# Fourier mixing and a squared-ReLU layer: a seven-product scheme for most groups, sums and casts by DMA

## The chip, the cores and the metric

The kernel runs on one core of a Trainium2 chip. The metric is the device time of one launch in microseconds, the median of several runs. The profile shows one execution in detail: TensorE (PE, with its weight loads as PEld), VectorE (DVE), ScalarE (ACT), GpSimd (POOL), SyncE (SP) and the DMA queues.

## The reference

```python
# x: (8, 3008, 256); filt_r, filt_i: (1505, 256); w_in: (256, 2048); w_out: (2048, 256)
def _attn_ref(x, filt_r, filt_i):
    X = np.fft.rfft(x, axis=1)
    F = (filt_r + 1j * filt_i)[None, :, :]
    return np.fft.irfft(X * F, n=x.shape[1], axis=1).astype(np.float32)

def _moe_ref(x, w_in, w_out):                     # x: the result above, 24064 rows of 256
    h = np.maximum(x @ w_in, 0.0)
    return (h * h @ w_out).astype(np.float32)
```

Each of the 8 sequences is filtered in the frequency domain, and the 24064 rows that result go through two layers with the square of a ReLU between them.

## The kernel before

The discrete Fourier transform of 3008 = 64 x 47 points is made of matrix products with constant matrices in f16. For each sequence `b` it runs in steps: `unit_a` (16 units: transforms of 47 points), a way out to DRAM and back that changes the layout (`write_u`, `read_u`), `unit_b` (12 units: transforms of 64 points, times the filter), `unit_p` (12 units: back), again through DRAM (`read_z`), and `unit_y` (16 units), which leaves the filtered sequence in `yts`. x comes in as f32 and is cast to f16:

```python
def load_x(b, c, pool=None, tag="x32", q=None):
    t = (pool or p_x32).tile([96, 8, D], F32, tag=tag, name=f"x32_{b}_{c}")
    q = q or nc.sync
    ...
    x32s[(b, c)] = t

def cast_x(b, c, eng=nc.vector):
    t = p_x16.tile([94, 8, D], F16, tag="x16", name=f"x16_{b}_{c}")
    eng.tensor_copy(out=t, in_=x32s.pop((b, c))[0:94])
    x16s[(b, c)] = t
```

`unit_b` multiplies each pair of rows by both parts of the filter. `prod[:, 0]` and `prod[:, 1]` are the two halves of the complex product; the second has to be added with its upper and lower 64 partitions exchanged:

```python
def unit_b(b, p):
    ps = psF(...)                                   # psF: a ring of two PSUM banks
    for i in range(2):
        nc.tensor.matmul(ps[:, i * D:(i + 1) * D], sSB[:, 2 * p + i, :],
                         uts[b][:, 2 * p + i, :], start=True, stop=True)
    prod = p_prod.tile([128, 2, 2, D], F16, tag="prod", name=f"prod_{b}_{p}")
    nc.vector.tensor_mul(out=prod, in0=<ps, each element twice>, in1=sF[:, :, 2 * p:2 * p + 2, :])
    if b > 0:
        yf = p_yf.tile([128, 2, D], F16, tag="yf", name=f"yf_{b}_{p}")
        nc.vector.tensor_copy(out=yf[0:64], in_=prod[64:128, 1])
        nc.vector.tensor_copy(out=yf[64:128], in_=prod[0:64, 1])

def unit_s(b, p):
    prod, yf = prods[(b, p)]
    nc.vector.tensor_add(out=yf, in0=prod[:, 0], in1=yf)

def unit_p(b, p):
    ps = psF(f"psP_{b}_{p}")
    for i in range(2):
        nc.tensor.matmul(ps[:, i * D:(i + 1) * D], sSP[:, 2 * p + i, :], yf[:, i, :], start=True, stop=True)
    nc.scalar.copy(out=zes[(b, c)][:, 2 * i6:2 * i6 + 2, :], in_=ps...)
    ...
```

The two layers run in 47 groups of 512 rows, each in 8 slots. In slot `s` of group `g` the first layer makes two of its 16 blocks of `h2` (2048 x 512, f16), ScalarE takes the ReLU out of PSUM and VectorE squares it; beside this the second layer of the group before is computed, and units of the Fourier part are strewn in by a plan:

```python
def ffn_g1(g, s):
    for i in range(2):
        jt = 2 * s + i
        ...
        nc.tensor.matmul(ps[:, i, o:o + n], sWin[:, dt, jt * 128:(jt + 1) * 128], yts[b][:, dt, r:r + n], ...)
    nc.scalar.activation(out=h2[:, 2 * s:2 * s + 2, :], in_=ps, func=AF.Relu)

def ffn_sq(g, s):
    v = h2s[g][:, 2 * s:2 * s + 2, :]
    nc.vector.tensor_mul(out=v, in0=v, in1=v)

def ffn_g2(g, s):                                   # direct: 8 products of 256 columns a slot
    t, half = divmod(s, 2)
    for jt in range(8 * half, 8 * half + 8):
        nc.tensor.matmul(pso[g][:, t % 2, :], h2s[g][:, jt, t * 128:(t + 1) * 128],
                         sWout[:, jt, :], start=(jt == 0), stop=(jt == NJT - 1))
```

For groups 40 to 45 the second layer uses Strassen's scheme in Winograd's form instead: h2 and w_out are seen as 2 x 2 blocks, four sums of blocks of h2 (`sums`, in slots 0, 1, 2 and 4) and four of w_out (`make_t`, once) leave seven block products in place of eight. `products` computes them in parts over the 8 slots, 14 matmuls of 128 columns in each on average, and puts the results together:

```python
def sums(g, k):                                     # k = 0, 1, 2, 4
    t = p_x16.tile([128, 8, D], F16, tag="x16", name=f"sum_{g}_{k}")
    if k == 0:
        nc.vector.tensor_add(out=t, in0=a21, in1=a22)
    ...

def products(g, k):
    for p, m0, m1 in PARTS[k]:
        ...
        for m in range(m0, m1):
            q, t = divmod(m, 2)
            nc.tensor.matmul(o[:, t, :], f[p][:, q, 128 * t:128 * t + 128], sg["w"][p][:, q, :], ...)
        if p == 1:
            f["pu"] = p_prod.tile([128, 2, 2, 128], F32, tag="prod", name=f"pu_{g}")
            nc.scalar.copy(out=f["pu"][:, 0], in_=o)
        ...
        elif p == 2:
            nc.vector.tensor_add(out=f["top"][:, :, 0:128], in0=f["y"][:, 0], in1=f["pu"][:, 0])
            nc.vector.tensor_add(out=f["bot"][:, :, 128:256], in0=f["y"][:, 1], in1=f["pu"][:, 1])
        ...
        elif p == 3:
            nc.vector.tensor_add(out=f["top"][:, :, 128:256], in0=o, in1=f["u2"])
            store(g, 0, 2, f["top"])
```

The plan of a sequence (`b` > 1; `first` is a multiple of 8 slots) and the loop:

```python
t0 = 6                                              # unit_a: two a slot, slots 6 to 13
put(14, 1, read_u, b)
t0 = 19
for p in range(12):                                 # unit_b: 12 over 19 slots, unit_p two slots later
    r = t0 + 18 * p // 11
    put(r, 0, unit_b, b, p)
    put(r, 0, unit_s, b, p)
    put(r + 2, 1, unit_p, b, p)
for c in range(4):
    put(40, 1, read_z, b, c)
...                                                 # load_x and cast_x of the next sequence
for n in range(16):                                 # unit_y: two a slot, slots 45 to 52
    put(45 + n // 2, n % 2, unit_y, b, n)

SEVEN = range(40, NG - 1)
for s in range((NG + 1) * SLOTS):
    g, k = divmod(s, SLOTS)
    if g < NG: ffn_g1(g, k)
    run(work, s, 0)
    if (s - 1) // SLOTS - 1 in SEVEN: products((s - 1) // SLOTS - 1, (s - 1) % SLOTS)
    if g > 0 and g - 1 not in SEVEN: ffn_g2(g - 1, k)
    run(work, s, 1)
    ...
    if g - 1 in SEVEN: sums(g - 1, k)
    if g < NG: ffn_sq(g, k)
```

Of the kernel before, what the change touches and what calls it, by code (L numbers as in the profile page):

```python
# [110 lines left out]
def kernel(  # L111
# [32 lines left out]
    p_prod = ctx.enter_context(tc.tile_pool(name="p_prod", bufs=3))  # L144
    p_yf = ctx.enter_context(tc.tile_pool(name="p_yf", bufs=4))
# [3 lines left out]
    p_out = ctx.enter_context(tc.tile_pool(name="p_out", bufs=3))  # L149

# [33 lines left out]
    x32s = {}  # L184

    def load_x(b, c, pool=None, tag="x32", q=None):

        t = (pool or p_x32).tile([96, 8, D], F32, tag=tag, name=f"x32_{b}_{c}")
        q = q or nc.sync
        if b + 1 < B:  # L190
            v = xrows[b * S:b * S + 96 * NM, :].rearrange("(p m) d -> p m d", m=NM)
            q.dma_start(out=t, in_=v[:, 8 * c:8 * c + 8, :])
        else:
            v = xrows[b * S:b * S + S, :].rearrange("(p m) d -> p m d", m=NM)
            q.dma_start(out=t[0:80], in_=v[0:80, 8 * c:8 * c + 8, :])
            q.dma_start(out=t[80:94], in_=v[80:94, 8 * c:8 * c + 8, :])
        x32s[(b, c)] = t
# [3 lines left out]
    sC0 = const.tile([128, 1472], F16, name="sC0")  # L201
# [3 lines left out]
    sSA = sC0[0:94, 1280:1376]  # L205
    sSY = sC0[0:112, 1376:1470]
# [40 lines left out]
    nc.sync.dma_start(out=sC0[:, 704:1472], in_=dC0.ap()[:, 704:1472])  # L247
# [60 lines left out]
    def load_win():  # L308

        for k, c, n, pool, tag in ((0, 0, 768, p_ze, "ze"), (0, 768, 768, p_ze, "ze"),  # L310
                                   (0, 1536, 512, p_prod, "prod"), (1, 0, 768, p_ze, "ze"),
                                   (1, 768, 512, p_prod, "prod"), (1, 1280, 512, p_prod, "prod"),
                                   (1, 1792, 256, p_yf, "yf")):
            t = pool.tile([128, n], F32, tag=tag, name=f"win32_{k}_{c}")
            nc.sync.dma_start(out=t, in_=moe_w_in[128 * k:128 * k + 128, c:c + n])
            wins.append((t, k, slice(c, c + n)))
# [19 lines left out]
    x16s, us, uts, prods, zes, zts, yts = {}, {}, {}, {}, {}, {}, {}  # L336

    def cast_x(b, c, eng=nc.vector):
        t = p_x16.tile([94, 8, D], F16, tag="x16", name=f"x16_{b}_{c}")
        eng.tensor_copy(out=t, in_=x32s.pop((b, c))[0:94])  # L340
        x16s[(b, c)] = t

# [5 lines left out]
    def unit_a(b, a):  # L348

        c, i = divmod(a, 4)  # L350
        if i == 0:
            us[(b, c)] = p_u.tile([96, 8, D], F16, tag="u", name=f"u_{b}_{c}")
        ps = psF(f"psA_{b}_{a}")
        m = slice(2 * i, 2 * i + 2)
        if b == 1:
            nc.tensor.matmul(ps[0:96, :], s1[:, c // 2, :], xw16[(b, 2 * (c % 2))][:, m, :],
                             start=True, stop=False)
            nc.tensor.matmul(ps[0:96, :], s1[0:120, 2 + c, :], xw16[(b, 1)][0:120, m, :],
                             start=False, stop=True)
        else:  # L360
            nc.tensor.matmul(ps[0:96, :], sSA, x16s[(b, c)][:, m, :], start=True, stop=True)  # L361
        o = us[(b, c)][:, 2 * i:2 * i + 2, :]
        pv = ps[0:96, :].rearrange("p (a d) -> p a d", d=D)
        if a % 2 == 0:
            nc.scalar.copy(out=o, in_=pv)  # L365
        else:
            nc.vector.tensor_copy(out=o, in_=pv)  # L367
        if i == 3:
            write_u(b, c)
# [69 lines left out]
    def unit_b(b, p):  # L439
# [18 lines left out]
        if b > 0:  # L458
            yf = p_yf.tile([128, 2, D], F16, tag="yf", name=f"yf_{b}_{p}")
            nc.vector.tensor_copy(out=yf[0:64], in_=prod[64:128, 1])  # L460
            nc.vector.tensor_copy(out=yf[64:128], in_=prod[0:64, 1])
            prods[(b, p)] = prod, yf

    def unit_s(b, p):

        prod, yf = prods[(b, p)]
        nc.vector.tensor_add(out=yf, in0=prod[:, 0], in1=yf)  # L467
        prods[(b, p)] = yf
# [20 lines left out]
    def unit_p(b, p):  # L489
# [3 lines left out]
        yf = prods.pop((b, p))  # L493
# [12 lines left out]
    ztiles = [const.tile([112, 8, D], F16, name=f"zt_{c}") for c in range(4)]  # L506
# [3 lines left out]
    def read_z(b, c, ks=(0, 1)):  # L510
        zt = ztiles[c]
        v = dZ[b].rearrange("(q j) d -> q j d", j=NM)
        for k in ks:
            nc.sync.dma_start(out=zt[64 * k:64 * k + 48],
                              in_=v[48 * k:48 * k + 48, 8 * c:8 * c + 8, :])
        zts[(b, c)] = zt
# [51 lines left out]
    def ffn_sq(g, s):  # L568
        v = h2s[g][:, 2 * s:2 * s + 2, :]
        nc.vector.tensor_mul(out=v, in0=v, in1=v)  # L570
# [46 lines left out]
    def make_t():  # L617

        t = p_x32.tile([128, 4, 8, 128], F16, tag="x32", name="sT")
# [13 lines left out]
    def sums(g, k):  # L633
# [7 lines left out]
        t = p_x16.tile([128, 8, D], F16, tag="x16", name=f"sum_{g}_{k}")  # L641
# [17 lines left out]
    def products(g, k):  # L659

        f = sg[g]
        for p, m0, m1 in PARTS[k]:
# [12 lines left out]
            if p == 1:  # L675
                f["pu"] = p_prod.tile([128, 2, 2, 128], F32, tag="prod", name=f"pu_{g}")
                nc.scalar.copy(out=f["pu"][:, 0], in_=o)
            elif p == 6:
                f["u2"] = p_prod.tile([128, 2, 128], F32, tag="prod", name=f"u2_{g}")
                nc.scalar.copy(out=f["u2"], in_=o)  # L680
            elif p == 7:
                nc.scalar.copy(out=f["pu"][:, 1], in_=o)
            elif p == 2:
                f["top"] = p_out.tile([128, 2, 256], F32, tag="ost", name=f"top_{g}")
                f["bot"] = p_out.tile([128, 2, 256], F32, tag="ost", name=f"bot_{g}")
                nc.vector.tensor_add(out=f["top"][:, :, 0:128], in0=f["y"][:, 0], in1=f["pu"][:, 0])
                nc.vector.tensor_add(out=f["bot"][:, :, 128:256], in0=f["y"][:, 1], in1=f["pu"][:, 1])
            elif p == 4:
                nc.scalar.copy(out=f["bot"][:, :, 0:128], in_=o)
                store(g, 2, 2, f["bot"])  # L690
            elif p == 3:
                nc.vector.tensor_add(out=f["top"][:, :, 128:256], in0=o, in1=f["u2"])
                store(g, 0, 2, f["top"])

    def fft_plan(b):
# [11 lines left out]
        t0 = 2 if b == 1 else 6  # L707
        for a in range(12 if b == 1 else 0, 16):
            put(t0 + a // 2, a % 2, unit_a, b, a)
        put(10 if b == 1 else 14, 1, read_u, b)  # L710
        t0 = 14 if b == 1 else 19
        for p in range(12):
            r = t0 + (17 if b == 1 else 18) * p // 11
            put(r, 0, unit_b, b, p)
            put(r, 0, unit_s, b, p)
            put(r + 2, 1, unit_p, b, p)
        t0 = 34 if b == 1 else 40
        for c in range(4):
            put(t0, 1, read_z, b, c)
        if b + 1 < B:  # L720
            for c in range(2):
                put(t0 - 13, 1, load_x, b + 1, c)
            for c in range(4):
                r = t0 - 8 + 3 * c
                put(r, 1, cast_x, b + 1, c)
                if c < 2:
                    put(r, 1, load_x, b + 1, c + 2)
# [79 lines left out]
    SEVEN = range(40, NG - 1)  # L807
    work = {}
    for b in range(1, B):
        first = (b * S // TG) * SLOTS - (48 if b > 1 else 40)  # L810
        for (r, place), w in fft_plan(b).items():
            work[(first + r, place)] = w
# [49 lines left out]
```

## Time and profile before

| | |
|---|---|
| median of 3 runs | 789.52 us (789.43 to 789.87) |
| span of the profiled execution | 787.2 us |
| granted TensorE clock | 1.00 throughout |
| ReLU on ScalarE (L566) | 376 x 1025 ns |
| first layer on TensorE (L562) | 1728 matmuls |
| second layer, direct (L579) | 2624 matmuls of 256 columns |
| second layer, seven products (L670) | 672 matmuls of 128 columns |
| squares on VectorE (L570) | 376 x 684 ns |
| DMA, mean over the span | 136 GB/s |

In the lines of the profile, L562 and the like are lines of the kernel; `h<-psH` names what is written and what is read; then come the shape, how often, the busy time in all and the mean duration in ns, and the idle time of the engine before such instructions with what ended it. A matmul's duration contains its way through the pipeline, so matmuls overlap, and the busy time of TensorE says less than the distance between their starts.

### The profile page before, as it was taken

The numbers are of one execution on the slowest core, as the hardware profiler recorded it, in microseconds if no ns is written. First come the engines' busy times: TensorE is split into PE (matmuls) and PEld (weight loads), VectorE is DVE, ScalarE is ACT, GpSimd is POOL, SyncE is SP. The second block draws the span as 40 slices with busy tenths as digits, with TensorE's granted clock in tenths as the row PEclk, the third lists the DMA queues.
The fourth block names the chain that finished last, engine by engine and source line by source line (L and its number), as shares of the span: only waits on it lengthen the run. The fifth ranks groups of instructions, "written<-read, shape, count | busy, mean of one in ns | idle before, by whom it ended". The sixth has DMA issues, their size and how long they took to land.

```text
span 787.2 us, 15477 instructions
## 1 busy us (share of the span) xinstructions
PE 774.9 (98%) x6390; PEld 552.6 (70%) x6390; DVE 584.4 (74%) x943; ACT 558.5 (71%) x723; POOL 23.6 (3%) x36
## 2 busy tenths in 40 slices
PE   8989999999999999999999999999999999999998
PEld 5846667667676676867778677776767667677776
DVE  6866995579855897559965599556995569878884
ACT  3976776777777776767776777676777767777674
POOL 3800000000000000000000000000000000000000
PEclk9999999999999999999999999999999999999999
DMA  9995554345724467054571555525564342421011
GB/s 363 371 258 157 147 158 112 88 139 158 193 67 109 158 169 181 32 160 145 134 186 49 169 141 140 148 67 161 147 169 98 91 138 82 109 67 54 29 54 55
DMA packets 88574, 107.36 MB, mean 136 GB/s; under 512 B 6336, under 2 KB 79040, under 8 KB 84288
## 3 DMA queue, kind: packets, MB, share of 16 engines
q1 hardware_dynamic: 88296, 106.19, 46.9%
q8 instruction: 50, 0.82, 0.4%
q10 hardware_dynamic: 144, 0.18, 0.1%
q14 instruction: 20, 0.16, 0.1%
q0 software_dynamic: 64, 0.00, 0.0%
HBM read 58.12 MB, written 48.23 MB: 135 GB/s over the span
## 4 chain that ended last, share of the span: by engine, by line
PE 91%; DVE 6%; ACT 1%; DMA 1%; issue 0%; ACTq 0%; SPq 0%; DVEq 0%
PE psH L562 39%; PE psO L579 34%; PE psX L670 3%; PE psA L361 3%; PE psY L532 2%; PE psB L445 2%; PE psP L496 2%; PE psY L670 2%; DVE prod L453 2%; DVE h L570 2%; PE warm L268 1%; DMA wout<-in_moe_w_out_dram 1%; PE psf L287 1%; PE psf L290 1%; DVE yf L467 0%; ACT sF L298 0%
## 5 line engine op out<-in xcount | busy, mean ns | idle before, releaser
L566 ACT ACTIVATE h<-psH 128x1024 f16<-128x1024 f32 x376 | 384.9, 1025 | 183.1 <-PE psH L562 180.5
L562 PE MATMUL psH<-yt,sWin 128*128 128x512 f16 (+7 forms) x1728 | 386.9, 351 | 1.7 <-DVE yt L541 0.7
L579 PE MATMUL psO<-sWout,h 128*128 128x256 f16 x2624 | 339.2, 272 | 0.6 <-DVE h L570 0.6
L570 DVE TENSOR_TENSOR h<-h 128x1024 f16<-128x1024 f16 x376 | 251.9, 684 | 66.3 <-ACT h L566 65.6
L579 PEld LDWEIGHTS <-h 128*128 128x128 f16 x2624 | 253.3, 98 | 66.0 <-DVE h L570 0.9
L562 PEld LDWEIGHTS <-sWin 128*128 128x128 f16 x1728 | 157.7, 98 | 100.7 <-issue 3.4
L453 DVE TENSOR_TENSOR prod<-psB,sF 128x1024 f16<-128x1024 f32 x84 | 102.3, 1218 | 2.8 <-PE psB L445 2.7
L541 DVE CAST yt<-psY 128x376 f16<-128x376 f32 x62 | 34.0, 549 | 54.7 <-PE psY L532 54.6
L367 DVE CAST u<-psA 96x512 f16<-96x512 f32 x50 | 34.3, 687 | 47.3 <-PE psA L361 45.1
L498 ACT CAST ze<-psP 128x512 f16<-128x512 f32 x84 | 49.1, 585 | 17.2 <-PE psP L496 14.7
L590 ACT COPY ost<-psO 128x512 f32<-128x512 f32 (+1 forms) x84 | 48.8, 581 | 7.7 <-PE psO L579 4.3
L532 PE MATMUL psY<-sC,zt 112*128 112x94 f16 x512 | 42.3, 205 | 1.0 <-DMA zt<-dZ 1.0
L532 PEld LDWEIGHTS <-zt 112*128 112x128 f16 x512 | 34.9, 98 | 11.1 <-issue 1.2
L467 DVE TENSOR_TENSOR yf<-prod,yf 128x512 f16<-128x512 f16 x84 | 35.7, 425 | 2.9
L361 PE MATMUL psA<-x,sC 94*96 94x512 f16 x96 | 36.6, 382 | 0.0
L445 PE MATMUL psB<-ut,sSB 128*128 128x256 f16 x192 | 36.5, 273 | 0.0
L496 PE MATMUL psP<-yf,sSP 128*128 128x256 f16 x168 | 32.1, 272 | 0.5 <-DVE prod L453 0.3
L445 PEld LDWEIGHTS <-sSB 128*128 128x128 f16 x192 | 18.5, 98 | 19.5
L539 ACT CAST yt<-psY 128x376 f16<-128x376 f32 x66 | 30.9, 468 | 1.6 <-issue 1.3
L340 DVE CAST x<-x 94x2048 f16<-94x2048 f32 x24 | 29.2, 1216 | 0.0
L365 ACT CAST u<-psA 96x512 f16<-96x512 f32 x50 | 28.6, 572 | 0.0
L670 PEld LDWEIGHTS <-sum 128*128 128x128 f16 x384 | 23.8, 98 | 4.9
(88 smaller groups left out, 395.3 us busy)
## 6 DMA issues: line engine op xcount, KB each, us to landing
x<-in_x_dram SPq DMA_DIRECT2D x20, 768.0 KB
zt<-dZ SPq DMA_DIRECT2D x64, 192.0 KB
dU<-u SPq DMA_DIRECT2D x28, 384.0 KB
dZ<-ze SPq DMA_DIRECT2D x28, 384.0 KB
out_dram<-ost SPq DMA_DIRECT2D x58, 128.0 KB
ut<-dU SPq DMA_DIRECT2D x7, 1024.0 KB
out_dram<-ost SPq DMA_DIRECT2D x27, 256.0 KB
xw<-in_x_dram SPq DMA_DIRECT2D x6, 1024.0 KB
```

Source lines behind the costliest of these rows:

```text
L361: nc.tensor.matmul(ps[0:96, :], sSA, x16s[(b, c)][:, m, :], start=True, stop=True)
L445: nc.tensor.matmul(ps[:, i * D:(i + 1) * D], sSB[:, 2 * p + i, :], uts[b][:, 2 * p + i, :], start=True, stop=True)
L453: nc.vector.tensor_mul(out=prod, in0=ps.rearrange("p (a d) -> p a d", d=D).unsqueeze(1).to_broadcast([128, 2, 2, D]), in1=sF[:, :, 2 * p:2 ...
L496: nc.tensor.matmul(ps[:, i * D:(i + 1) * D], sSP[:, 2 * p + i, :], yf[:, i, :], start=True, stop=True)
L498: nc.scalar.copy(out=zes[(b, c)][:, 2 * i6:2 * i6 + 2, :], in_=ps.rearrange("p (a d) -> p a d", d=D))
L532: nc.tensor.matmul(ps[:, 94 * jj:94 * jj + 94], zt[:, 4 * (g % 2) + jj, dt * 128:(dt + 1) * 128], sSY, start=True, stop=True)
L562: nc.tensor.matmul(ps[:, i, o:o + n], sWin[:, dt, jt * 128:(jt + 1) * 128], yts[b][:, dt, r:r + n], start=(dt == 0), stop=(dt == 1))
L566: nc.scalar.activation(out=h2[:, 2 * s:2 * s + 2, :], in_=ps, func=AF.Relu)
L570: nc.vector.tensor_mul(out=v, in0=v, in1=v)
L579: nc.tensor.matmul(pso[g][:, t % 2, :], h2s[g][:, jt, t * 128:(t + 1) * 128], sWout[:, jt, :], start=(jt == 0), stop=(jt == NJT - 1))
L590: nc.scalar.copy(out=ost[:, h0:h0 + step, :], in_=pso[g][:, h0:h0 + step, :])
L670: nc.tensor.matmul(o[:, t, :], f[p][:, q, 128 * t:128 * t + 128], sg["w"][p][:, q, :], start=(m == 0 and p in (1, 2)), stop=(q == 7), skip ...
```

## The change

The seven-product scheme is used for groups 9 to 45 in place of 40 to 45. It gives TensorE fewer columns to stream and gives VectorE sums to form. To make room on VectorE, three kinds of its work change:

- the exchanged half of the complex product is added by two DMAs that accumulate into `prod[:, 0]`, issued from GpSimd, in place of two copies and an addition; `unit_p` comes four slots after `unit_b` in place of two;
- x is loaded by DMAs from GpSimd that cast to f16 on the way, in place of a load and a cast on VectorE;
- a square covers two slots (2048 elements a partition) in place of one.

Buffers move to make room: the sums of the scheme lie in the tiles that held x in f32, `top` and `bot` collect their parts in place, the blocks of w_out take the place of constants no longer needed, and there are three tiles `zt` in place of four, so that the last part of Z is read six slots later. The starts of the stages in the plan shift by a slot.

```diff
+            nc.gpsimd.dma_start(out=t, in_=v[:, m, :])          # load_x: f32 in DRAM, f16 tile
...
-    def cast_x(b, c, eng=nc.vector):
-        t = p_x16.tile([94, 8, D], F16, tag="x16", name=f"x16_{b}_{c}")
-        eng.tensor_copy(out=t, in_=x32s.pop((b, c))[0:94])
-        x16s[(b, c)] = t
...
         if b > 0:
-            yf = p_yf.tile([128, 2, D], F16, tag="yf", name=f"yf_{b}_{p}")
-            nc.vector.tensor_copy(out=yf[0:64], in_=prod[64:128, 1])
-            nc.vector.tensor_copy(out=yf[64:128], in_=prod[0:64, 1])
-            prods[(b, p)] = prod, yf
-
-    def unit_s(b, p):
-
-        prod, yf = prods[(b, p)]
-        nc.vector.tensor_add(out=yf, in0=prod[:, 0], in1=yf)
-        prods[(b, p)] = yf
+            for i in range(2):
+                nc.gpsimd.dma_start(out=prod[64 * i:64 * i + 64, 0],
+                                    in_=prod[64 - 64 * i:128 - 64 * i, 1],
+                                    accum_op=mybir.AluOpType.add)
...
-    ztiles = [const.tile([112, 8, D], F16, name=f"zt_{c}") for c in range(4)]
+    ztiles = [const.tile([112, 8, D], F16, name=f"zt_{c}") for c in range(3)]
...
     def ffn_sq(g, s):
-        v = h2s[g][:, 2 * s:2 * s + 2, :]
+        n = 1 if g == NG - 1 else 2
+        if (s + 1) % n:
+            return
+        v = h2s[g][:, 2 * (s + 1 - n):2 * s + 2, :]
         nc.vector.tensor_mul(out=v, in0=v, in1=v)
...
-        t = p_x16.tile([128, 8, D], F16, tag="x16", name=f"sum_{g}_{k}")
+        if k in (0, 2):
+            f["s"] = p_x32.tile([128, 2, 8, D], F16, tag="x32", name=f"sum_{g}_{k}")
+        t = f["s"][:, 0 if k in (0, 2) else 1]
...
-        t0 = 2 if b == 1 else 6
+        t0 = 2 if b == 1 else 5
...
-        t0 = 14 if b == 1 else 19
+        t0 = 14 if b == 1 else 18
         for p in range(12):
-            r = t0 + (17 if b == 1 else 18) * p // 11
+            r = t0 + (15 if b == 1 else 18) * p // 11
             put(r, 0, unit_b, b, p)
-            put(r, 0, unit_s, b, p)
-            put(r + 2, 1, unit_p, b, p)
-        t0 = 34 if b == 1 else 40
+            if b + 1 < B and 2 <= p < 10:
+                put(r, 0, load_x, b + 1, p - 2)
+            put(r + 4, 1, unit_p, b, p)
+        t0 = 34 if b == 1 else 41
         for c in range(4):
-            put(t0, 1, read_z, b, c)
+            put(t0 if c < 3 else t0 + 6, 1, read_z, b, c)
...
-    SEVEN = range(40, NG - 1)
+    SEVEN = range(9, NG - 1)
```

## The prediction, made blind

> **What bounds the kernel now.** I read the page's busy times first, then the waits, then the order of work in single stretches.
>
> ```profile
> PE 774.9 (98%) x6390; PEld 552.6 (70%) x6390; DVE 584.4 (74%) x943; ACT 558.5 (71%) x723; POOL 23.6 (3%) x36
> ...
> ACT h L566 <- PE psH L562: 180.5, 347, 1.1
> DVE h L570 <- ACT h L566: 65.6, 74, 2.0
> ...
> PE psH L562 <- DVE yt L541: 0.7, 2, 0.5
> ```
>
> The last three lines are from the view of waits (us in total, times, longest). ScalarE and VectorE wait for TensorE; TensorE hardly ever waits for them. So TensorE bounds the kernel, and its time is the columns that it streams. Busy time alone would not prove that, since matmul records overlap; what proves it is that the slots of the loop keep an even beat. One slot is one eighth of a group of 512 tokens: four 512-column matmuls of the first layer and an eighth of the second layer. Rows of the timeline (start, duration in us):
>
> ```profile
> 682.43 1.03 PE L562 MATMUL psH<-yt,sWin 128*128 128x512 f16 x4
> ...
> 689.38 1.03 PE L562 MATMUL psH<-yt,sWin 128*128 128x512 f16 x4
> ...
> 725.45 1.06 PE L670 MATMUL psX<-sWout,h 128*128 128x128 f16 x16
> ...
> 738.61 1.06 PE L670 MATMUL psX<-sWout,h 128*128 128x128 f16 x16
> ```
>
> The first two rows are four slots apart, without Fourier work, with the direct second layer: 6.95 / 4 = 1.737 us a slot, 13.90 a group. The other two are one whole group apart in the last stretch, where the before kernel already has the seven-product scheme: 13.16 us a group, 1.645 a slot. **The scheme is therefore worth 0.74 us a group**, measured on this chip in this kernel, as long as nothing else gets in the way.
>
> What could get in the way is VectorE. Busy time by stretch (span, PE, PEld, DVE, ACT):
>
> ```profile
> core 0: us, PE busy (x) PEld busy (x) DVE busy (x) ACT busy (x) POOL busy (x), PEclk, DMA share, GB/s
> 600.67:611.12 10.45, 10.45 (x125) 8.68 (x122) 5.74 (x10) 7.92 (x14) 0.00 (x0) 1.00 0.11 35
> 615.06:628.13 13.07, 13.07 (x90) 8.62 (x89) 7.71 (x12) 9.93 (x15) 0.00 (x0) 1.00 0.33 87
> 640.94:677.00 36.06, 36.06 (x262) 25.44 (x260) 34.83 (x63) 26.84 (x34) 0.00 (x0) 1.00 0.25 80
> 682.43:689.38 6.95, 6.95 (x50) 4.70 (x48) 4.25 (x7) 4.69 (x6) 0.00 (x0) 1.00 0.93 235
> 725.45:751.77 26.32, 26.32 (x289) 18.77 (x288) 21.61 (x31) 18.66 (x24) 0.00 (x0) 1.00 0.13 43
> ```
>
> These are, in order: the last transform (unit_y), the first (unit_a), the middle of the Fourier part (unit_b and unit_p), slots without Fourier work, and seven-product groups without Fourier work. In the third, VectorE is busy 34.8 of 36.1 us: full already, and only just not the bound. The seven-product scheme alone takes 82% of it (21.6 of 26.3). Both at once would not fit; so the change frees VectorE at the same time.
>
> **What the Trainium skill says.** "VectorE: DVE Perf Modes", section "The perf-mode tier table", puts a 16-bit tensor_tensor of 2048 elements at 1224 ns; the sums here take 1218 ns (row below), so it agrees. "TensorE: Matmul & The Clock Gate", section "Back-to-back issue gap", gives about 81 ns for each matmul of 128 columns with its own weights in a sustained stream; here 16 of them follow a 512-column block within 0.89 us (725.45 to 726.34), 56 ns each. The measurement decides: the weight loads are hidden. "DMA: Bandwidth & Descriptors", section "SWDGE vs HWDGE vs iDMA", says that casts and accumulation in a DMA must be issued from GpSimd, which builds their descriptors in software; the section "Anatomy of one DMA" gives about 2 us fixed per such DMA. The trace has only two small ones, 0.62 and 0.48 us of GpSimd each, landing after 6.2 us in the crowded prologue. "SBUF — State Buffer", section "SBUF: two separate sides", warns that GpSimd and VectorE share an SBUF port pair and can hold up each other; no row here shows it.
>
> **The change part by part.**
>
> ```profile
> L570 DVE TENSOR_TENSOR h<-h 128x1024 f16<-128x1024 f16 x376 | 251.9, 684 | 66.3 <-ACT h L566 65.6
> L453 DVE TENSOR_TENSOR prod<-psB,sF 128x1024 f16<-128x1024 f32 x84 | 102.3, 1218 | 2.8 <-PE psB L445 2.7
> L467 DVE TENSOR_TENSOR yf<-prod,yf 128x512 f16<-128x512 f16 x84 | 35.7, 425 | 2.9
> L643 DVE TENSOR_TENSOR sum<-h 128x2048 f16<-128x2048 f16 x6 | 7.3, 1216 | 0.0
> ```
>
> (1) Seven products for groups 9 to 45 instead of 40 to 45: 31 more groups. TensorE: 31 x 0.74 = **22.8 us less**. VectorE gains per group four sums of 1.218 and three additions of 0.42 us, 6.1 us; 31 x 6.1 = 190 us. ScalarE gains four copies of 0.37 and loses two of 0.59: +0.3 us a group, 9 us in all.
>
> (2) The complex products: two half copies (24.3 and 24.1 us in all, L460 and L461) and the addition L467 (35.7) leave VectorE: 84 us less. In their place 7 x 24 accumulating DMAs of 64 rows by 1 KB. Their result is wanted by unit_p, which moves from two slots after unit_b to four.
>
> (3) x is cast by its DMA: the 24 casts (29.2 us, L340) leave VectorE. Eight loads a sequence go out from GpSimd instead, between the accumulating DMAs.
>
> (4) Squares over two slots: a group goes from 8 x 0.684 to 4 x 1.218, 0.6 us less; 46 groups, 28 us. A square then ends later, but it is wanted two slots later.
>
> (5) Moved buffers (sums in the old x32 tiles, T in the place of the constants, three zt tiles, top and bot filled in place): they free memory; the last read of Z goes out six slots later and still four slots, some 8 us, before its use.
>
> VectorE in sum: 584 - 84 - 29 - 28 + 190 = **633 us, 82%** of some 770. Over the whole span it fits. By stage it is tight. Instructions in a full VectorE queue start closer than their durations: L643 at 725.13, the square at 726.26, L646 at 726.86, so 1.13 us for the long ones and 0.60 for the short. Eight slots with the middle Fourier part then want 4 squares and 4 sums (9.0), three additions (1.05) and 5.05 products (12 in 19 slots) of 1.14 (5.8): 15.9 us. TensorE wants 8 x 1.645 and 5.05 x 0.43 for unit_b and unit_p (slots with both are 2.17 apart instead of 1.74): 15.3 us. **VectorE is 0.5 us over per eight slots**, 1.2 us over the 19 slots. The stages of unit_y (13.9 against 16.0) and unit_a (15.0 against 16.7) fit, with a crowd in slots 0 and 1 of a group, where two sums and a square come together.
>
> I walked the order of the queues by hand through 19 slots of the middle part, with a square ready 2.1 us after its slot starts and a product 1.28 us after. The squares and sums keep their dates; what fails is one psF bank: unit_b's sixth matmul pair finds the product of the fifth not done and waits 0.75 us. Then the queues run in step. Groups without Fourier work (10.1 of 13.2 us) absorb the rest. Five sequences (3 to 7) have this stage under the scheme: 5 x 0.75 = 3.8 us given back. A product is done 5.3 to 7.5 us before unit_p wants its sum. Two accumulating DMAs take an estimated 1.1 us of GpSimd (the two issues of the trace) and the fixed 2 us of the skill: they land in time, if they aren't held up.
>
> Sum: 789.5 - 22.8 + 3.8 = 770.5; 1.5 us more for waits that a walk with fixed durations doesn't have: **772.0 us**.
>
> **The rivals.** (a) VectorE becomes the bound in every Fourier stage: instructions wait for semaphores instead of following at 1.13 us. If they take 1.22, eight slots want 1 us more, up to 2.5 us per sequence, 5 to 12 us in all: 775 to 782. For it: 34.8 of 36.1 today. Against: TensorE lost nothing there today.
> (b) The accumulating DMAs are late, because GpSimd and VectorE hold up each other, or stand behind a casting load of x, which comes between them: at the 6.2 us of the prologue some unit_p would wait, and if 9 us were usual, 2 to 4 us per sequence in seven sequences: 785 to 795. For it: no such DMA has run in this kernel outside the prologue. Against: four slots look chosen with a margin, and the DMA share there is 0.25.
> (c) Nothing waits: 789.5 - 22.8 = 766.7.
>
> **Range and chances.** The result lies between (c) and the upper half of (a), more likely near the lower end: 765.5 to 783.0. Faster by 2% means under 773.7: my sum lies 1.7 us below, so 0.58; within 2% 0.36, for (a) and a mild (b); slower 0.06, for a strong (b).
>
> **What would show each step.** Right: a group of eight slots without Fourier work 13.16 us from group 9 on; VectorE near 633 us busy; ScalarE near 568; new waits of TensorE for VectorE of some 4 to 6 us, in the middle stage, at psB. Wrong: TensorE waiting for the accumulating DMAs before psP (rival b), durations of sums and squares above 1.22 us (the shared port), or slots in the stages of unit_y and unit_a that are longer than 2.0 and 2.1 us.

## The result and the profile after

The changed kernel takes **783.28 us** (median of 4 runs, 781.18 to 784.45) against 789.56 us for the kernel before, a ratio of 0.992 (interval 0.989 to 0.994). The predicted 772.0 us was 11 us too low.

In the kernel after, L553 is the first layer's matmul, L666 those of the seven products, L564 the square, L450 the complex product, L457 the accumulating DMA, L195 the casting load of x. From its page (a group's columns: busy us, mean ns, idle time before it and who ended it):

```profile
PE 755.4 (97%) x7878; PEld 552.5 (71%) x7878; DVE 627.2 (80%) x699; ACT 561.6 (72%) x785; POOL 193.0 (25%) x260
...
L457 POOL DMA_DIRECT2D prod<-prod x168 | 141.1, 997 | 463.7 <-DVE prod L450 458.4
...
L642 DVE TENSOR_TENSOR sum<-sum,h 128x2048 f16<-128x2048 f16 x37 | 45.2, 1221 | 0.9
```

VectorE went from 584 to 627 us with 244 instructions fewer, and the sums last as long as before. From the view of waits (us in total, times, longest):

```profile
ACT h L557 <- PE psH L553: 170.3, 355, 1.4
DVE h L564 <- ACT h L557: 64.3, 49, 2.9
...
PE psY L666 <- DVE bot L681: 5.5, 5, 1.2
PE psY L523 <- DMA zt<-dZ: 4.9, 7, 1.4
...
PE psP L487 <- DMA prod<-prod: 2.6, 4, 0.7
```

ScalarE and VectorE still wait for TensorE most of the time. Of the last three lines the first and the third are new, and the second was one single wait of 1.0 us in the prologue before: TensorE now waits for an addition on VectorE, for the way of Z through DRAM and for an accumulating DMA. Busy time by engine in three stretches: the 18 slots of the middle stage of sequence 4 in the kernel before, the same 18 slots in the kernel after, and two groups without Fourier work in the kernel after:

```profile
core 0: us, PE busy (x) PEld busy (x) DVE busy (x) ACT busy (x) POOL busy (x), PEclk, DMA share, GB/s
354.17:390.02 35.85, 35.85 (x261) 25.25 (x259) 34.22 (x60) 26.55 (x34) 0.00 (x0) 1.00 0.52 148
...
349.46:384.99 35.53, 34.29 (x367) 25.14 (x365) 34.79 (x35) 25.34 (x36) 20.79 (x28) 1.00 0.82 154
705.00:731.32 26.32, 26.32 (x291) 18.77 (x289) 20.90 (x23) 18.70 (x25) 0.00 (x0) 1.00 0.13 41
```

The last row is 13.16 us a group: the scheme's gain is there. The first two rows show where it goes. The same 18 slots took 35.85 us before and take 35.53 now, with TensorE idle for 1.2 us of them and VectorE busy for all but 0.7.

**How much was waited.** I took the starts of successive matmuls and subtracted the columns streamed, at 2.4 columns a ns (a 512-column matmul lasts 379 ns, one of 256 columns 272). Distances over by more than 0.25 us, from group 7 to 46, sum to 0.0 us before and 15.5 us after. That closes the account: the span before, 787.2, minus 22.8, plus 15.5, makes 779.9, and the profiled span is 780.7.

The 15.5 us are three waits that come back from sequence to sequence, and one of 0.6 us for U: the additions hold TensorE once in each of the sequences 3 to 7, the sums once in 3, 4 and 5 and three times in 6, Z once in each of 2 to 7. **First wait**, 0.9 to 1.4 us at slot 7 of the middle stage's first group (timeline: start, duration, engine, line):

```profile
358.57 1.22 DVE L564 TENSOR_TENSOR h<-h 128x2048 f16<-128x2048 f16 x1
359.71 1.22 DVE L450 TENSOR_TENSOR prod<-psB,sF 128x1024 f16<-128x1024 f32 x1
359.79 0.61 PE L666 MATMUL psX<-sT,h 128*128 128x128 f16 x8
360.84 0.41 DVE L681 TENSOR_TENSOR top<-psY,top 128x256 f32<-128x256 f32 x1
361.17 0.41 DVE L681 TENSOR_TENSOR bot<-psY,bot 128x256 f32<-128x256 f32 x1
361.64 0.38 PE L666 MATMUL psY<-sWout,sum 128*128 128x128 f16 x4 [1.24 <-DVE bot L681]
```

The product p = 3 accumulates in `y[:, 1]`, which the second addition of p = 2 must have read before. The additions stand in VectorE's queue behind a square and a complex product, so TensorE stops for 1.24 us here, 1.4 by the count of starts. **Second wait**, late in the middle stage, for the accumulating DMAs:

```profile
376.58 1.14 POOL L195 DMA_DIRECT2D x<-in_x_dram  x1
378.47 0.81 POOL L457 DMA_DIRECT2D prod<-prod  x1 [0.74 <-DVE prod L450]
380.28 0.81 POOL L457 DMA_DIRECT2D prod<-prod  x1 [1.00 <-issue]
380.80 0.83 POOL L195 DMA_DIRECT2D x<-in_x_dram  x1
381.33 1.97 POOL L457 DMA_DIRECT2D prod<-prod  x2
...
387.75 0.38 PE L487 MATMUL psP<-prod,sSP 128*128 128x256 f16 x2 [0.73 <-DMA prod<-prod]
```

The load of x issued at 380.80 landed at 386.68; the two accumulating DMAs issued after it, at 381.33 and 381.85, landed at 387.15 and 387.61, and unit_p waited for them. **Third wait**, at the first unit_y of a sequence:

```profile
393.96 1.83 SPq L606 DMA_DIRECT2D out_dram<-bot  x3
395.10 0.58 ACT L489 CAST ze<-psP 128x512 f16<-128x512 f32 x1
395.88 0.40 SPq L604 DMA_DIRECT2D out_dram<-top  x1
396.38 0.44 SPq L492 DMA_DIRECT2D dZ<-ze  x1
396.91 5.15 SPq L505 DMA_DIRECT2D zt<-dZ  x6
...
403.10 0.33 PE L523 MATMUL psY<-sC,zt 112*128 112x94 f16 x4 [0.52 <-DMA zt<-dZ]
```

The last unit_p lies one slot later than before (40 in place of 39), unit_y still starts at 45. Its values have five slots of 1.645 us, 8.2 us, in place of six of 1.737, 10.4 us, to get to DRAM and back. The write of Z also stands behind output stores in SyncE's queue: `ze` is ready at 395.68 and the write goes out at 396.38.

### The profile page after: what moved, and what is told of

Same layout as the page of the kernel before. It is cut to its first block, busy times and chain, and to the rows that moved or that the text cites. A ratio compares the mean times of both kernels' runs of the same rounds, so it can differ in the third digit from the quotient of the medians.

```text
span 780.7 us, 18857 instructions
## 1 busy us (share of the span) xinstructions
PE 755.4 (97%) x7878; PEld 552.5 (71%) x7878; DVE 627.2 (80%) x699; ACT 561.6 (72%) x785; POOL 193.0 (25%) x260
## 5 line engine op out<-in xcount | busy, mean ns | idle before, releaser
L553 PE MATMUL psH<-yt,sWin 128*128 128x512 f16 (+7 forms) x1728 | 386.9, 351 | 1.5 <-DVE yt L532 0.5
L564 DVE TENSOR_TENSOR h<-h 128x2048 f16<-128x2048 f16 (+1 forms) x192 | 229.6, 1196 | 64.8 <-ACT h L557 64.3
L457 POOL DMA_DIRECT2D prod<-prod x168 | 141.1, 997 | 463.7 <-DVE prod L450 458.4
L553 PEld LDWEIGHTS <-sWin 128*128 128x128 f16 x1728 | 153.4, 98 | 98.5 <-issue 3.4
L666 PEld LDWEIGHTS <-sum 128*128 128x128 f16 x2368 | 146.8, 98 | 27.2 <-issue 6.1
L666 PEld LDWEIGHTS <-h 128*128 128x128 f16 x1776 | 110.3, 98 | 22.5
L450 DVE TENSOR_TENSOR prod<-psB,sF 128x1024 f16<-128x1024 f32 x84 | 102.4, 1219 | 14.4 <-PE psB L442 14.4
L666 PE MATMUL psX<-sT,sum 128*128 128x128 f16 x1184 | 84.2, 219 | 0.0
L573 PE MATMUL psO<-sWout,h 128*128 128x256 f16 x640 | 81.8, 272 | 0.0
L573 PEld LDWEIGHTS <-h 128*128 128x128 f16 x640 | 62.0, 98 | 14.6 <-issue 0.2
L666 PE MATMUL psY<-sT,sum 128*128 128x128 f16 x592 | 57.2, 219 | 0.0
L666 PE MATMUL psY<-sWout,sum 128*128 128x128 f16 x592 | 44.9, 219 | 5.5 <-DVE bot L681 5.5
L195 POOL DMA_DIRECT2D x<-in_x_dram x40 | 46.1, 1151 | 0.0
L642 DVE TENSOR_TENSOR sum<-sum,h 128x2048 f16<-128x2048 f16 x37 | 45.2, 1221 | 0.9
L666 PE MATMUL psY<-sWout,h 128*128 128x128 f16 x592 | 45.2, 219 | 0.0
L666 PE MATMUL psX<-sT,h 128*128 128x128 f16 x592 | 45.1, 219 | 0.0
```

Of the source, the lines that this page charges most:

```text
L195: nc.gpsimd.dma_start(out=t, in_=v[:, m, :])
L450: nc.vector.tensor_mul(out=prod, in0=ps.rearrange("p (a d) -> p a d", d=D).unsqueeze(1).to_broadcast([128, 2, 2, D]), in1=sF[:, :, 2 * p:2 ...
L457: nc.gpsimd.dma_start(out=prod[64 * i:64 * i + 64, 0], in_=prod[64 - 64 * i:128 - 64 * i, 1], accum_op=mybir.AluOpType.add)
L642: nc.vector.tensor_sub(out=t, in0=f[5], in1=a11)
```

## The experiments

The theory: each of the three waits is one of order or of date, and costs what it shows. Its rivals: the load of VectorE as such is the cause (VectorE is full, so the order can't matter); or GpSimd's DMAs are (rival (b) of the prediction), so that the loads of x are what must go; or the relief itself costs time, whatever the scheme brings. All edits are made to the kernel after, and ratios are to the kernel before.

### e1_adds_first: the additions earlier in the queue

```diff
-        run(work, s, 0)
+        early = (s - 1) % SLOTS == 5          # the slot in which p = 2 ends
+        if not early: run(work, s, 0)
         ...products(...)
+        if early: run(work, s, 0)
-    for v, i in ((top, 0), (bot, 1)):         # the two additions of p = 2
+    for v, i in ((bot, 1), (top, 0)):
```

> In the slots in which product p=2 is finished, the block products are issued ahead of unit_b, so that VectorE does the two additions before the next complex product, and the addition that product p=3 waits for goes first. Theory A (VectorE's full queue holds the additions, and p=3 may not write its bank before): the five waits of 0.9 to 1.4 us before psY for p=3, 6.4 us in all, shrink below 1.5 us in all; the time falls by 4 to 6 us, to about 778. Rival (VectorE is simply over its time in this stage, wherever the wait shows): the waits move to psB or psP a few slots later, and the time falls by less than 2 us.

Measured: 780.40 us (778.75 to 782.02), ratio 0.988 (0.986 to 0.990). The first wait fell from 6.4 to 2.4 us in sum, at the same load of VectorE: it is a matter of order. But the other two waits took all of it back, 3.3 us at unit_p (4.1 to 7.4) and 1.1 us at Z, so that this execution waits for 15.4 us in all, as the kernel after. The median is 2.9 us lower, but the two intervals touch; what fits is that TensorE comes earlier to sums and to a Z that are as late as before.

### e2_x_earlier: the loads of x ahead of the middle stage

```diff
-            if b + 1 < B and 2 <= p < 10:
-                put(r, 0, load_x, b + 1, p - 2)
+            if b == 1 and 2 <= p < 10: put(r, 0, load_x, b + 1, p - 2)
+            elif 1 < b < B - 1 and p < 8: put(7 + p, 0, load_x, b + 1, p)
```

> From sequence 2 on, the casting loads of x go out in slots 7 to 14 of the plan, right after unit_a has freed each tile, and not between the accumulating DMAs. Theory B (the accumulating DMAs stand behind the loads of x in GpSimd's queue): the waits for prod before psP, 4.1 us in all, vanish, an accumulating DMA lands 2.3 to 3.6 us after its issue even for the late units, and the time falls by 3 to 4 us, to about 780. Rival (the sums are late because the products are late on VectorE): the waits before psP stay, and the time stays within 1 us. A new wait of unit_b for ut would show that the loads crowd the way of U through DRAM instead.

Measured: 793.12 us (788.62 to 798.48), ratio 1.004 (1.0025 to 1.005). All six waits of unit_p are gone, as they should be without loads between the sums; one new one of 1.6 us has come, at the last unit_p of sequence 4 (see e11). But the loads now run beside the way of U through DRAM, and unit_b waits for it; the view of waits has it as

```profile
PE psB L442 <- DMA ut<-dU: 14.6, 5, 4.3
```

Five waits, one in each of the sequences 2 to 6, are 15.4 us by the count of starts, against 2.5 us less at unit_p, and the clock makes them dearer (last section).

### e3_z_from_act: the last write of Z from ScalarE's queue

```diff
-            nc.sync.dma_start(out=dZ[b]...)
+            (nc.scalar if c == 3 else nc.sync).dma_start(out=dZ[b]...)
```

> The last write of Z of a sequence is issued from ScalarE's queue, right behind the copy that fills it, and not from SyncE's, where it stands behind the stores of the output. Theory C (the way of Z through DRAM has too few slots): the write goes out 0.6 to 1.0 us earlier, the waits for zt before psY, 4.8 us in all, fall to 1 us or less, and the time falls by 3 to 4 us, to about 780. Rival (the reads themselves are slow because the DMA queues are crowded): the wait stays above 3 us and the time within 1 us.

Measured: 780.06 us (779.05 to 783.50), ratio 0.988 (0.986 to 0.990). The timeline shows the write no longer behind the store:

```profile
395.32 0.58 ACT L489 CAST ze<-psP 128x512 f16<-128x512 f32 x1
395.93 0.37 ACTq L492 DMA_DIRECT2D dZ<-ze  x1
396.15 0.40 SPq L604 DMA_DIRECT2D out_dram<-top  x1
```

0.03 us from the end of the copy to the issue, where it was 0.70. The waits for Z fell from 4.5 to 2.1 us, all waits from 15.5 to 12.5; the interval of the time still touches that of the kernel after.

### e4_all_three: the edits of e1, e2 and e3 together

> All three edits together. If the three causes are apart from each other, the waits of TensorE after the prologue fall from 17 to 3 us or less, and the time to 769 to 772. If VectorE is simply over its time in the middle stage, waits of more than 1 us per sequence appear elsewhere, and the time stays above 775.

Measured: 787.05 us (783.34 to 791.67), ratio 0.996 (0.995 to 0.998), where 769 to 772 was expected. All three waits are small (2.1, 1.8 and 1.0 us); 14.2 us of waiting for U remain from e2. The loads of x must not lie there.

### e5_x_late and e6_adds_xlate_zact: the loads of x behind the middle stage

```diff
+            elif 1 < b < B - 1 and p < 8: put(46 + p, 1, load_x, b + 1, p)    # e6: with e1 and e3
```

> From sequence 2 on, the casting loads of x go out in slots 46 to 53 of the plan: behind the accumulating DMAs, the way of U and all but the last read of Z. Theory B in its second form (the loads hold up whichever transfer shares their slots, first the accumulating DMAs, in the run with early loads the way of U): the waits before psP fall from 4.1 to 1.6 us or less, no wait of more than 0.5 us comes up before psB, and the time falls by 2 to 4 us, to 779 to 781. If a wait before psY or psA comes up instead, the loads have no free place in this plan.

> The late loads of x, the additions ahead of the complex product, and the last write of Z from ScalarE, together. If the three causes are apart: the waits of TensorE after the prologue fall from 17 to 6 us or less, and the time to 770 to 774. If VectorE is over its time in the middle stage whatever the order, the time stays above 776 with waits at psB or psP that follow late products.

Measured: 819.57 us, ratio 1.037 (1.036 to 1.039), and 819.73 us, 1.037 (1.036 to 1.039). I had expected the loads to start when the plan names them. The timeline of e5 shows otherwise:

```profile
406.34 3.71 POOL L195 DMA_DIRECT2D x<-in_x_dram  x6
410.23 1.02 POOL L195 DMA_DIRECT2D x<-in_x_dram  x2 [0.18 <-issue]
411.55 0.38 SPq L492 DMA_DIRECT2D dZ<-ze  x1
412.01 11.24 SPq L505 DMA_DIRECT2D zt<-dZ  x6
...
424.69 0.47 PE L523 MATMUL psY<-sC,zt 112*128 112x94 f16 x4 [6.24 <-DMA zt<-dZ]
```

After its last accumulating DMA nothing blocks GpSimd's queue, so all eight loads go out at once, ahead of the write of Z, and Z waits behind them: 33.6 us in all. The waits of e5 grew by 27 us against the kernel after and the time by 36; the rest fits the clock, which is at half for 2.7 to 5.0 us after each of the five long waits, 21.3 us in all: an estimate of 10.6 us lost. Where a load stands in the plan is no date.

### e9_x_gated and e10_adds_xgated_zact: the same with a gate

```diff
+        if 1 < b < B - 1:
+            put(47, 1, gate, b)       # GpSimd copies two elements that unit_y of slot 47 writes
+            for k in range(8): put(47 + k // 2, 1, load_x, b + 1, k)       # e10: with e1 and e3
```

> The casting loads of x behind a gate: from sequence 2 on, GpSimd first copies two elements that the fifth unit_y has written, and issues the eight loads only then, in slot 47 of the plan. In the run with ungated late loads GpSimd had run ahead of the plan and put them on the way of Z. Theory B (the loads hold up whichever transfer shares their slots; slots 47 to 53 have only stores and one read of Z): the waits before psP fall from 4.1 to 2 us or less, the waits before psY stay below 5 us and no wait comes up before psB or psA; the time falls by 2 to 4 us against the change, to 779 to 781. Rival (no place is free): new waits before psA or psB above 3 us, time 785 or more.

> Gated loads of x, additions ahead of the complex product, last write of Z from ScalarE, together. If the three causes of waiting are apart from each other: waits of 6 us or less after the prologue and 770 to 774. If VectorE is over its time in the middle stage in any order: waits move to psB or psP, and the time stays above 776.

Measured: 790.96 us, ratio 1.001 (1.000 to 1.002), and 784.86 us, 0.992 (0.989 to 0.995). The gate holds the loads back, but the last reads of Z, planned for slot 47, now lie among them: TensorE waits for Z for 12.9 and 8.2 us, 8.3 and 7.1 of them at slot 51, which needs that last read. The six waits of unit_p are gone here too; one of 1.9 us has come at the last unit_p of sequence 4. None of the three other places tried for the loads was better than that of the change.

### e7_relief_alone: the old range of groups, everything else changed

```diff
-    SEVEN = range(9, NG - 1)
+    SEVEN = range(40, NG - 1)
```

> The whole change except for its first part: seven products for groups 40 to 45 only, as before. If the waits come from VectorE being full and from slots that are shorter than the DMAs' ways were planned for, they need the seven products: 789 to 791, with less than 2 us of waits after the prologue. If the adding and casting DMAs cost waits by themselves: 793 or more, with waits before psP and psY like those of the change.

Measured: 789.67 us (789.13 to 791.5), ratio 1.000 (0.999 to 1.001). TensorE's waits by my count are 0.3 us. The accumulating DMAs, the casting loads, the squares over two slots and the shifted plan cost nothing by themselves; the three waits come only beside seven products.

### e8_sums_on_vector: the sums back on VectorE

```diff
-            for i in range(2): nc.gpsimd.dma_start(out=<half of prod[:, 0]>, ..., accum_op=add)
+            yf = uts[b][:, 2 * p:2 * p + 2, :]
+            nc.vector.tensor_copy(out=yf[0:64], in_=prod[64:128, 1])
+            nc.vector.tensor_copy(out=yf[64:128], in_=prod[0:64, 1])
+            nc.vector.tensor_add(out=prod[:, 0], in0=prod[:, 0], in1=yf)
```

> The change with the complex products summed by VectorE again (two half copies and an addition, the exchanged half going through rows of ut that are no longer needed). VectorE's want in eight slots of the middle stage rises from 15.9 to about 21 us against 15.3 of TensorE. Theory (VectorE then bounds that stage in the five sequences with seven products): 8 to 12 us more per sequence, 825 to 840 in all, with VectorE busy without a gap in the stage. If the accumulating DMAs were the greater evil: 785 or less.

Measured: 869.21 us, ratio 1.100 (1.098 to 1.102). From the view of waits:

```profile
PE psY L666 <- DVE bot L681: 42.8, 15, 4.1
PE psB L442 <- DMA ut<-dU: 11.9, 6, 2.9
```

The expectation, 825 to 840 us, was far too low, and "busy without a gap" did not come: the 18 slots of the middle stage of sequence 4 take 49.5 us in place of 35.5, with VectorE busy for 45.6 of them and a mean clock of 0.90. So the run shows that the sums could not have stayed on VectorE in this form, but not how dear VectorE alone would be. Two other things go in: without accumulating DMAs to wait for, GpSimd sends the loads of x early, into the way of U (10 us at psB by my count); and the kernel is 11 us behind already where group 7 starts (170.5 us in place of 159.1), before any group of seven products.

### e11_no_x: the loads of x for sequences 3 to 7 left out

```diff
-            nc.tensor.matmul(ps[0:96, :], sSA, x16s[(b, c)][0:94, m, :], ...)
+            nc.tensor.matmul(ps[0:96, :], sSA, x16s[(2, c)][0:94, m, :], ...)
```

Five sequences compute on the x of sequence 2, so the output is another one; all other work is the same.

> The change with the casting loads of x for sequences 3 to 7 left out; these sequences use the x of sequence 2, so the output is another. Theory B: no wait before psP above 2 us in all, an accumulating DMA lands after 3 us or less in the median; the waits before psY for zt fall too if the loads crowd them, to 3 us or less; time 778 to 780. Rival (late products, not the loads, make the sums late): the waits before psP stay near 4 us and the time within 1 us of the change.

Measured: 781.67 us, ratio 0.990 (0.988 to 0.992), which overlaps the interval of the kernel after. All six waits of unit_p in the kernel after are gone: the loads were their cause. The 2.0 us in the table are one new wait, at the last unit_p of sequence 5, for an accumulating DMA that landed 4.55 us after its issue with no load of x in flight. One such wait, of 1.6 to 2.0 us at the last unit_p of sequence 4 or 5, comes in every run without loads between the sums (e2, e4, e5, e6, e9, e10, e11, e13) and in no other; why is not shown. The waits for additions (7.0) and for Z (5.2) grew. The loads delay the sums, but hardly the kernel.

### e12_adds_zact and e13_adds_zact_no_x: e1 and e3 together

> The additions ahead of the complex product and the last write of Z from ScalarE, with the loads of x where the change has them. Each alone took 3 us off. If they are apart: 777 to 778. If time freed in one place is taken back by the sums that now come too late for psP and by Z (both ways through DMA have a length in us, not in slots): 779 to 781, with more than 6 us of waits before psP.

> As the run before, and the loads of x for sequences 3 to 7 left out (their x is that of sequence 2, so the output is another). All three causes are then taken away without a load in another place. If the three causes are all there is: waits of 6 us or less after the prologue and 770 to 774. If not, the waits stay near 10 us and the time above 776, and the shorter slots themselves are what the DMAs' ways do not fit.

Measured: **775.35 us** (773.63 to 777.54) for e12, ratio 0.982 (0.980 to 0.984): faster than both kernels, with two small edits of order, and faster than either expectation. With the loads of x left out besides (another output, as in e11) 774.51 us, 0.981 (0.980 to 0.983), which can't be told from e12. The waits are down from 15.5 to 7.0 us; e1 and e3, whose medians alone were about 3 us lower each, give 8 together, and this interval lies clear of theirs and of that of the kernel after. The counts fit that one gain is no longer eaten by the next wait (unit_p 3.8 us here, 7.4 in e1), but they come from one execution of each kernel. In the timeline of e12 the additions come before the complex product:

```profile
355.55 1.22 DVE L564 TENSOR_TENSOR h<-h 128x2048 f16<-128x2048 f16 x1
356.68 0.42 DVE L681 TENSOR_TENSOR bot<-psY,bot 128x256 f32<-128x256 f32 x1
357.02 0.42 DVE L681 TENSOR_TENSOR top<-psY,top 128x256 f32<-128x256 f32 x1
357.35 1.22 DVE L450 TENSOR_TENSOR prod<-psB,sF 128x1024 f16<-128x1024 f32 x1
358.48 1.22 DVE L564 TENSOR_TENSOR h<-h 128x2048 f16<-128x2048 f16 x1
```

VectorE's queue is as full as ever (the long ones follow at 1.13 us); only who stands in front has changed. The 18 slots of sequence 4 show it:

```profile
346.43:381.31 34.88, 34.41 (x367) 25.09 (x365) 34.78 (x36) 25.31 (x36) 20.78 (x28) 1.00 0.84 159
```

VectorE is busy for all but 0.1 us, and the stage takes 34.9 us (34.8 to 35.7 in the five sequences), where TensorE by the slots of the prediction wants 18 x 1.645 + 12 x 0.43 = 34.8. What is left in its view of waits:

```profile
PE psP L487 <- DMA prod<-prod: 1.6, 3, 0.7
PE psY L523 <- DMA zt<-dZ: 1.5, 3, 1.0
PE psP L487 <- DVE prod L450: 1.2, 3, 0.7
...
PE psY L666 <- DVE top L681: 0.6, 2, 0.4
```

### e14_adds_zact_y46 and e15_sums_five_slots: one slot more for Z, or for the sums

```diff
-            put((38 if b == 1 else 45) + n // 2, n % 2, unit_y, b, n)
+            put((38 if b == 1 else 46) + n // 2, n % 2, unit_y, b, n)      # e14, on top of e12; the last read of Z moves along
...
-            put(r + 4, 1, unit_p, b, p)
+            put(r + (5 if b > 2 and p < 9 else 4), 1, unit_p, b, p)        # e15, on top of e12
```

> As the run with additions first and Z from ScalarE, and from sequence 2 on unit_y (and the last read of Z) one slot later, which gives the way of Z 1.6 us more. If that way is too long for its slots: the waits before psY for zt fall below 1 us in all, and the time by 1 to 2 us against the run without it. If the first layer then waits for yt (the next sequence's first columns are wanted in slot 48): new waits before psH of 0.4 us or more per sequence, and no gain.

> On top of additions first and Z from ScalarE: unit_p comes five slots after unit_b for the first nine units of sequences 3 to 7, and four slots after it for the last three, so that the way of Z starts when it did. If the summed products are just late by less than a slot: the waits before psP, 3.8 us in that run, fall below 1 us and the time by 2 to 3 us, to 772 to 773. If what is gained there is taken back by Z or by the additions: no change within 1 us.

Measured: 780.53 us, ratio 0.989 (0.987 to 0.990), and 779.06 us, 0.987 (0.985 to 0.988); both lose 4 to 5 us against e12. In e14 the wait for Z has gone from my count, but the first layer (2.6 us) and unit_a (1.6 us) now wait, as unit_y ends a slot later, and unit_p waits for 5.5 us in place of 3.8. In e15 two unit_p fall into one slot and the second waits for a PSUM bank; unit_p waits for 6.0 us. So neither of these two dates can be moved by a slot without another paying.

TensorE's waits by cause, in us over the span, by the count described above, one execution of each (without x: loads left out):

| kernel | time | all | additions (psY) | sums (psP) | Z (psY) | U (psB) |
|---|---|---|---|---|---|---|
| before | 789.56 | 0.0 | | | | |
| after | 783.28 | 15.5 | 6.4 | 4.1 | 4.5 | 0.6 |
| e1 | 780.40 | 15.4 | 2.4 | 7.4 | 5.6 | |
| e3 | 780.06 | 12.5 | 7.0 | 3.4 | 2.1 | |
| e12 | 775.35 | 7.0 | 2.0 | 3.8 | 0.9 | 0.3 |
| e11, without x | 781.67 | 14.2 | 7.0 | 2.0 | 5.2 | |
| e13, without x | 774.51 | 7.5 | 3.5 | 1.7 | 1.6 | 0.8 |
| e2 | 793.12 | 22.9 | 2.3 | 1.6 | 3.7 | 15.4 |
| e5 | 819.57 | 42.6 | 6.7 | 2.0 | 33.6 | 0.4 |
| e8 | 869.21 | 69.6 | 46.4 | 6.2 | 6.1 | 10.1 |

## Why the prediction was wrong

**The gain of 22.8 us was right** (it is 31 times the unrounded 0.734; 31 x 0.74 as written is 22.9). Groups without Fourier work take 13.16 us, and the account of the spans closes within 0.8 us with 22.8. VectorE (633 predicted) is busy for 627.2 us, ScalarE (568) for 561.6.

**The hand walk failed: the 3.8 us at psB.** By my count TensorE waited there once, for 0.6 us, and for U. The walk names squares, sums and products, and a psF bank; it does not name the bank in which the seven products themselves accumulate. There the additions of p = 2 must be read out before p = 3 may write, and a queue that is full delays exactly these short instructions: 6.4 us. e1 and e12 show it: the same instructions in another order, and the wait falls to 2.4 and 2.0 us. So the step "the squares and sums keep their dates; what fails is one psF bank" named the wrong bank.

**Part (5) failed: "still four slots, some 8 us, before its use".** It looked at the last read of Z. What TensorE waits for is the first, which needs all of Z written: the last unit_p went a slot later and unit_y did not. 4.5 us, and e3, which sends the write out 0.7 us earlier, takes 2.4 of them off.

**The landing of the sums was taken too low.** The step reads: "an estimated 1.1 us of GpSimd (the two issues of the trace) and the fixed 2 us of the skill: they land in time, if they aren't held up". A pair takes 1.64 us of GpSimd. The Trainium skill, "DMA: Bandwidth & Descriptors", section "Anatomy of one DMA", gives 2.0 us and the bytes at 436 GB/s, an estimate of 2.15 us for these 64 KB. Measured from issue to landing are 2.6 us in the median with no load of x in flight ahead (72 of them), and 4.2 us behind one (96), at most 7.4; the measurement decides. They were held up: against a margin of 5.3 to 7.5 us this was late often enough for 4.1 us, and with the loads gone (e11) all of these waits are gone. The DMA share of 0.25 that spoke against a hold-up was read in the last sequence (640.94 to 677.00), which has no x of a next one to load; the same stage of sequence 4 has 0.52 before and 0.82 after (rows above).

**The rivals.** (a) fell: full queues on VectorE follow at 1.13 us, as assumed, the durations of sums and squares did not grow, and in sequence 4 of e12 the stage runs at TensorE's own pace, 34.9 us, with VectorE as full. (b) was right in kind, sums late behind casting loads of x, but not in size: 4.1 us in place of 14 or more, and with the loads gone the interval of the time still overlaps that of the kernel after. (c) was not met even by e12; its 7.0 us of waits account for most of the 8.6 us that it lies above 766.7. The stages of unit_y and unit_a fit, as predicted: 1.96 and 2.06 us a slot in the mean of seven slots (sequence 4), and no wait but that for Z.

**The sum.** Predicted were 5.3 us given back (3.8 and 1.5), counted are 15.5; the 10.2 us between them are nearly the whole miss of 11.3. Three kinds of waits of 0.3 to 1.4 us did it, none of them visible in the busy time.

**Open.** Why the last 7 us of e12 remain, and whether another plan would remove them, is not settled; e14 and e15 show only that moving one date by a slot does not. The kernel after spreads over 3.3 us from run to run; the kernel before, measured again beside e1 to e4, over 2.1 (789.25 to 791.33 in 43 runs). A part of this shows: in the profiled executions of e2, e3, e7, e14 and e15 the clock stands at 0.50 for 3.4 us near 49 us, and group 7 starts at 160.4 to 160.6 us in place of 158.7 to 159.4. The rest is open.

## What to carry to other kernels

When a stage is filled to the brim, walk every bank and every buffer that is written again, those of the new scheme too, and every date that the change moves, not only the engine that was full before. Short instructions on which TensorE waits belong ahead of long ones that have slack; with one write moved to another queue this was worth 7.9 us here, more than the 6.3 of the change itself. Remove such waits together: one alone gave little here, and in e1 the other waits grew by as much as the first one fell. And read the load of a shared resource in a stretch that has all of its users.

## What the runs showed of the hardware

**A long wait can cost more than its length.** In e2 TensorE waited for 4.3 us for U, from 260.2 to 264.66. The windows of e2 around the end of that wait (columns as above; PEclk is the third last):

```profile
262.00:264.60 2.60, 0.00 (x0) 0.00 (x0) 0.00 (x0) 0.00 (x0) 0.00 (x0) 1.00 0.93 329
264.66:268.20 3.54, 3.54 (x21) 2.37 (x21) 2.36 (x2) 0.00 (x0) 1.42 (x2) 0.52 0.97 301
268.20:272.00 3.80, 3.80 (x43) 2.81 (x42) 3.40 (x3) 2.42 (x4) 1.91 (x3) 1.00 0.44 77
```

For the first 3.5 us after it the granted clock is 0.52, and 21 matmuls run where 43 run in the next 3.8 us. The Trainium skill, "TensorE: Matmul & The Clock Gate", section "What's actually happening", says that the clock falls to half after an idle window of about 3.4 us and stays there until a busy one. This trace agrees, but in other runs the clock fell after shorter waits. In e4 TensorE waited for 2.1 us, until 165.65, and the clock was half from 166.60 on:

```profile
166.60:170.00 3.40, 3.40 (x14) 1.83 (x13) 1.46 (x2) 1.02 (x1) 1.69 (x2) 0.50 0.75 231
```

A wait of 2.6 us in e2, until 360.72, left the clock at 1.00 in the 3.5 us after it. So the measurement decides: waits of 2.1 us and more were dearer in some cases and not in others, and those of the kernel after, at most 1.4 us, leave the clock at 1.00.

**GpSimd's DMAs went out when nothing ahead in its queue was waiting, not when the plan names them.** In sequences 3 and 4 of e5 loads planned for slots 46 to 53 went out in slots 38 to 41, in e8 loads planned for slots 21 to 32 in slots 7 to 13; the waits for Z came to 33.6 us in e5, those for U to 10 us in e8. An instruction with a real dependence (e9) held them back.
